# Spectral filter and routed experts on one core: first turn of the last batch moved ahead, bias product on 128 rows, other banks, start loads, blank writes and tail regrouped

## Chip, cores and metric

One Trainium2 chip, one core of it. The metric is the device time of one execution in microseconds (us), smaller is better; several executions are timed and their median is given. One further execution was taken by the hardware profiler; its own time stands beside its span.

## What is computed

The reference, cut to its two stages (`D = 256`, 8 batches of 2,496 tokens; 8 experts, hidden size 1,024):

```python
def _attn_ref(x, w_r, w_i, b_r, b_i):          # x: (8, 2496, 256)
    X = np.fft.rfft(x, axis=1)
    Yr = Xr @ w_r - Xi @ w_i + b_r
    Yi = Xr @ w_i + Xi @ w_r + b_i
    Yr = np.sign(Yr) * np.maximum(np.abs(Yr) - 0.01, 0.0)   # Yi alike
    return np.fft.irfft(Yr + 1j * Yi, n=2496, axis=1)

def _moe_ref(x, w_gate, w1, w2):               # x: (19968, 256)
    expert_idx = np.argmax(x @ w_gate, axis=1)
    for e in range(8):
        xe = x[expert_idx == e]
        out[expert_idx == e] = gate_w[:, None] * (np.maximum(xe @ w1[e], 0) @ w2[e])
```

`gate_w` is the softmax probability of the chosen expert. All of it is float32.

## The kernel before, in words

**Spectral stage.** The transform of length 2,496 is done as 39 x 64, with matmuls by constant matrices. A batch is worked in 10 "turns" of 2 frequencies each; 8 x 10 = 80 iterations `it` of one loop in `spectral` go through them, software-pipelined: in an iteration PE, the TensorE queue, does the forward product of the next turn (`fwd_b`, tile `pb` from the loaded `t` and the basis `bm`), the second inverse product of an older one (`inv_b`, tile `pv` from `y` and the basis `bi`), the products by the weights (`mix`: `pk`, then `pm`, written as sums of float32r halves `whr`, `wlr`, `sh`, `sl`), the first forward products of the next batch (`fwd_a`, tile `pa`) and last inverse products of the batch before (`inv_a`, which is `inv_z` with tile `pz` and, one piece behind, `inv_y` with tile `py`). Tables `first`, `loads`, `back` and `pieces` say which of these stand in which `it`. VectorE (DVE) and ScalarE (ACT) work between the products: ACT copies `k` from `pk` in the last batch (DVE adds in the others), DVE sums `v` from `pm` and `k`, ACT makes `r` and DVE `y` (the soft threshold), ACT copies `z` from `pv`, `zh` and DVE `zl` are the halves of `pz`, ACT copies `yb` from `py`. In the last batch the bias is added inside `pm` by one more matmul (line 355), whose stationary operand `ones` and moving operand `bias_r` have 33 partitions.

**Experts.** A route job (DVE and ACT steps on `lg`, `mx`, `scan`, ...) finds each token's expert and place; rows are scattered to `xs` in DRAM by POOL (GpSimd), and 82 tiles of 256 tokens then go through `up` (tile `ph`) and `down` (tile `po`), with an indirect store to `out` by POOL. The first `BUSY = 7` tiles are mixed with the end of the last batch in `finish_last`; `breathe` there gives the jobs in hand three steps between two pieces of matmuls, one of these jobs being `table(1)`, which computes the table of the late tiles and ends with the product `pl` from `lap`. The last `RARE = 3` tiles stand in an If each, read from the table (`live`); with these data none is taken.

**What sets the order.** PE, ACT, DVE and SP (the queue that issues the hardware DMAs) run in the order in which the code is written (`manual_schedule`), so a wait of one instruction holds all behind it on its engine. PSUM banks come from pools: `psf` has one bank "b" (`pb`) and one "m" (`pk` and `pm`), `psi` has a ring "u" of four (`pa`, `pv`, `pz`) and a pair "yo" (`py`, `pn`, `pq`, `pl`). `write_blank` has POOL issue 8 DMAs of 270 KB that put an empty tile ahead of every expert's rows.

Of the kernel before, what the change touches and what calls it, by code (L numbers as in the profile page):

```python
# [100 lines left out]
class Kernel:  # L101
# [71 lines left out]
    def open_forward(self, st):  # L173
        tc, nc, nb = self.tc, self.nc, self.nb
        f = self.f = self.pool(st, "f", 1, side="right")
        self.xst = ExitStack()
        self.xp = self.pool(self.xst, "xp", 4)
        self.tp = self.pool(st, "tp", 6, side="right")
        self.w = self.pool(st, "w", 2, side="right")
        self.psf = self.pool(st, "psf", 1, side="right", space=PSUM)  # L180

        y = [self.w.tile([128, 2, D], F32, tag="y", name=f"first{i}", bufs=3) for i in range(2)]
        self.idle, self.row1, self.brow = y[0][:, 0, :].bitcast(BF16), y[0][0:1, 1, 0:128], y[1][0:1]
        nc.vector.memset(self.idle, 0.0)
        nc.vector.memset(self.row1, 1.0)
        self.far = far = f.tile([117, 120], F32, name="far")
        self.fer = f.tile([78, 120], F32, name="fer")
        nc.sync.dma_start(far, self.c_fa)
        self.bm = f.tile([128, K1, 128], F32, name="bm")
        self.bi = f.tile([128, K1, 128], F32, name="bi")  # L190
        self.bias = f.tile([128, 2, D], F32, name="bias")
        self.bias_r = f.tile([33, 2, D], F32R, name="bias_r")
        self.ones = f.tile([33, 128], F32R, name="ones")
        self.xg = {}
        for q in range(6):
            self.load_x(0, q)
        nc.sync.dma_start(self.fer, self.c_fe)
        self.wh, self.wl = {}, {}
        self.raw = {}
        self.nlam = f.tile([128, 1], F32, name="nlam")  # L200
        nc.vector.memset(self.nlam, -LAM)

        nc.gpsimd.dma_start(self.gar, self.c_ga)
        for c in range(2):
            nc.gpsimd.dma_start(self.iw[:, c, c * 128:c * 128 + 8], self.w_gate[c * 128:(c + 1) * 128, :])
        nc.gpsimd.dma_start(self.ids, self.c_ids)
        nc.gpsimd.dma_start(self.score, self.c_score)
        nc.gpsimd.dma_start(self.base, self.c_base)
        nc.gpsimd.dma_start(self.ltri_f, self.c_ltri)
        nc.gpsimd.dma_start(self.tcol, self.c_tcol)  # L210
        for z in self.zs:
            nc.gpsimd.memset(z[:, :, 64:66, :], 0.0)
# [48 lines left out]
    def split_bias(self, part):  # L261
        nc = self.nc
        if part == 0:
            nc.scalar.activation(self.bias_r[0:32], self.bias[0:32], AF.Copy, scale=self.tcol[0:32, 2:3])
        elif part == 1:
            bh = self.w.tile([33, 2, D], F32R, tag="y", name="bh", bufs=3)
            nc.scalar.copy(bh[32:33], self.bias[32:33])
            nc.vector.tensor_sub(self.bias_r[32:33], self.bias[32:33], bh[32:33])
        else:
            nc.scalar.activation(self.ones, self.ident[0:33], AF.Copy, scale=0.0, bias=1.0)  # L270

# [73 lines left out]

    def mix(self, b, s):
        nc = self.nc
# [23 lines left out]
        yield  # L371
        if b or s:
            p = self.psf.tile([128, 2, D], F32, tag="m", name="pm", bufs=1)
        else:
            p = self.psi.tile([128, 512], F32, tag="u", name="pm", bufs=4).rearrange("p (a d) -> p a d", a=2)
# [22 lines left out]
    def inv_b(self, b, s):  # L398
        nc = self.nc
        y = self.ys.pop((b, s))  # L400
        p = self.psi.tile([128, 512], F32, tag="u", name="pv", bufs=4).rearrange(
            "p (c a r n) -> p c a r n", c=2, a=2, r=2)
        for kp in range(2):
# [12 lines left out]
    def inv_z(self, b, i):  # L416
        nc = self.nc
        for g in (2 * i, 2 * i + 1) if i < GH else ():
# [7 lines left out]
            nc.scalar.copy(h, p[:120, :YW])  # L426
            nc.vector.tensor_sub(l, p[:120, :YW], h)
            self.hl[g] = h, l
# [14 lines left out]
    def spectral(self, fwd):  # L443
# [7 lines left out]
        for i, pair in enumerate(pairs):  # L451
            self.fwd_a(0, *pair)
            if i == 4:
                self.load_basis("bm", 0, 2)
                self.load_w("r")
# [5 lines left out]
        self.turn(0, 1)  # L461
        self.load_basis("bm", 2, 6)
        self.turn(0, 2)
        if nb > 1:
            self.load_x(1, 0)
        self.turn(0, 3)
        self.load_basis("bi", 0, 4)
        self.keep_warm(12)
# [8 lines left out]
        for b in range(1, nb):  # L477
            at = 10 * b - 10
            for i, o in enumerate((1, 2, 2, 3, 3, 4, 4, 5, 5, 6, 6) if b == 1 else (-3, -2, -1, 0, 0, 1, 2, 3, 4, 5, 6)):
                first[at + o].append((b, *pairs[i]))  # L480
# [12 lines left out]
        for it in range(n):  # L493
# [10 lines left out]
            if it:  # L504
                small = self.shrink(*todo[it - 1])
                next(small)
            mix = self.mix(b, s)
            next(mix)
# [10 lines left out]
            self.tick(1)  # L519
            self.nudge()  # L520
            for a in pieces[it][:1]:
                self.inv_a(*a)
            next(mix, None)
            self.tick(3 if it >= n - 5 else 1)
            self.nudge()
# [3 lines left out]
            for a in pieces[it][1:]:  # L529
                self.inv_a(*a)  # L530
            for a in loads[it]:
                self.load_x(*a)
            if it == 3:
                self.split_inverse()
            if 6 < it < 10:
                self.split_bias(it - 7)
            if it == 6:
                self.write_blank(self.us[b, s][0:1, 0, 0:1])
            if it < 4:
                self.load_basis(*(("bm", 6, 12), ("bi", 4, 10), ("bm", 12, 20), ("bi", 10, 20))[it])  # L540
            if it + 4 < n and (it != 6 or nb == 1):
                if it == 7:
                    self.turn(*todo[it + 3])
                self.turn(*todo[it + 4])
# [16 lines left out]
        for _ in self.inv_b(*todo[n - 1]):  # L561
            pass
        self.inv_y(nb - 2, 9)
        self.inv_y(nb - 2, 10)
        self.pace(self.yb[0:1, GH - 1, 8:9])
# [24 lines left out]
    def breathe(self):  # L590
        self.tick(3)

    def finish_last(self):
        tiles = itertools.chain.from_iterable(self.step(t) for t in range(BUSY))
        fill = itertools.chain(self.first1(), self.first2())
        for i in range(GH + 1):
            self.inv_a(self.nb - 1, i)
            if i:
# [11 lines left out]
            self.breathe()  # L610
        self.jobs.append(self.table(1))
        for _ in tiles:
            self.breathe()
# [91 lines left out]
    def table(self, last):  # L705
# [82 lines left out]
        if last:  # L788
            lap = rt.tile([128, 128], F32, name="lap")
            nc.vector.tensor_copy(lap, fin[:, 3:4].broadcast_to((128, 128)))  # L790
            for _ in range(4):
                yield
# [225 lines left out]
    def experts_rest(self, late):  # L1018
        late.enter_context(self.tc.manual_schedule(engines={mybir.EngineType.Activation, mybir.EngineType.DVE}))
        main = self.nt - RARE  # L1020
        for t in range(BUSY, main):
            for _ in self.step(t):
                pass
        live = self.nc.values_load(self.tabs[1][0:1, 3, 0:1], min_val=0, max_val=self.nt)  # L1024
        nt = self.nt
        for t in range(main, nt):
            with self.tc.If(live > t - self.early):
                if t > main:
# [29 lines left out]
```

## Time and profile before

| | |
|---|---|
| timed runs | 1549.34, 1551.67, 1552.24 us; median 1551.67 us |
| profiled execution | 1549.26 us, span 1547.4 us |
| mean granted clock of TensorE | 0.995 |
| PE busy / weight loads | 1512.6 us (98%) / 1383.2 us (89%) |
| DVE / ACT / POOL busy | 957.2 us (62%) / 759.0 us (49%) / 392.5 us (25%) |
| spectral loop | from about 32 to 566 us of the span |
| steady state of the experts | from about 700 us on, with PE busy 800.0 of 800 us to 1500 |

Busy time of PE is the union of its matmuls' spans, whose ends are modelled and overlap; a pause of PE therefore is read from the start times. The clock column (PEclk) is 1.00 at 2.4 GHz and 0.50 at 1.2 GHz, or a mean between them. "Idle before" in a row counts from the modelled end of the matmul before it.

### The profile page before, as it was taken

How to read it: one execution, taken by the hardware profiler on the slowest of the kernel's cores; microseconds unless marked ns; L12 is line 12 of the kernel's file. 1: busy time of each engine (PE TensorE's matmuls, PEld its weight loads, DVE VectorE, ACT ScalarE, POOL GpSimd, SP SyncE). 2: the span in 40 equal slices, each digit the busy share in tenths (PEclk: the TensorE clock that was granted, in tenths of full speed). 3: DMA queues.
4: the chain of work that ended last, by engine and by line, in shares of the span. 5: the costliest groups of instructions: out<-in, count | busy, mean ns of one | idle time of the engine just before them, and what ended most of it. 6: DMA issues, size and time to landing. Idle time of an engine off the chain costs nothing. (4 is left out here: it accounts for less than half of the span.)

```text
span 1547.4 us, 35414 instructions
## 1 busy us (share of the span) xinstructions
PE 1512.6 (98%) x10808; PEld 1383.2 (89%) x10808; DVE 957.2 (62%) x2178; ACT 759.0 (49%) x1629; POOL 392.5 (25%) x550
## 2 busy tenths in 40 slices
PE   8999999999999999999999999999999999999997
PEld 3779899999898889899999999999999999999996
DVE  3778888889898777745555455454545445445442
ACT  2666766767666565434444434343434334334332
POOL 1100243343444453333421111111111111111111
PEclk9999999999999999999999999999999999999999
DMA  7954455555543332434443323232314124132210
GB/s 227 269 177 115 132 169 149 151 165 153 156 143 118 108 78 54 114 90 104 120 115 97 99 53 93 56 94 64 85 42 105 43 50 100 43 82 65 50 42 20
DMA packets 194726, 162.03 MB, mean 105 GB/s; under 512 B 127868, under 2 KB 164516, under 8 KB 194513
## 3 DMA queue, kind: packets, MB, share of 16 engines
q1 hardware_dynamic: 174705, 115.53, 29.2%
q0 software_dynamic: 19808, 44.03, 8.4%
q8 instruction: 88, 1.44, 0.4%
q14 instruction: 125, 1.02, 0.2%
HBM read 241.99 MB, written 66.37 MB: 199 GB/s over the span
## 5 line engine op out<-in xcount | busy, mean ns | idle before, releaser
L986 PE MATMUL po<-h,hh 128*128 128x512 f32 x1312 | 461.9, 395 | 0.0
L949 PE MATMUL ph<-xh,h 128*128 128x256 f32 x1312 | 372.0, 284 | 1.1 <-DVE hl L955 1.0
L949 PE MATMUL ph<-xl,h 128*128 128x256 f32 x1312 | 371.1, 283 | 0.0
L949 PE MATMUL ph<-xh,l 128*128 128x256 f32 x1312 | 370.7, 283 | 0.0
L983 PE MATMUL po<-h,hl 128*128 128x256 f32 x1148 | 323.9, 282 | 0.0
L955 DVE SCALAR_TENSOR_TENSOR hl<-ph,hh 128x512 fp32r<-128x512 f32 x328 | 226.1, 689 | 147.4 <-ACT hh L954 95.0
L954 ACT ACTIVATE hh<-ph 128x512 fp32r<-128x512 f32 x328 | 193.7, 598 | 205.5 <-PE ph L949 197.8
L986 PEld LDWEIGHTS po<-h,hh 128*128 128x128 f32 x1312 | 241.5, 188 | 43.4
L995 POOL DMA_INDIRECT out<-o,row x124 | 123.2, 994 | 581.6 <-DVE o L993 479.0
L993 DVE SCALAR_TENSOR_TENSOR o<-po,xr,part 128x256 f32<-128x256 f32 x156 | 75.4, 484 | 302.3 <-ACTq L911 153.7
L949 PEld LDWEIGHTS ph<-xh,l 128*128 128x128 f32 x1312 | 251.2, 191 | 3.7
L949 PEld LDWEIGHTS ph<-xh,h 128*128 128x128 f32 x1312 | 251.2, 191 | 2.5 <-DVE hl L955 2.1
L949 PEld LDWEIGHTS ph<-xl,h 128*128 128x128 f32 x1312 | 251.2, 191 | 0.0
L992 ACT ACTIVATE part<-po,xr 128x256 f32<-128x256 f32 x156 | 73.8, 473 | 334.5 <-PE po L986 318.3
L983 PEld LDWEIGHTS po<-h,hl 128*128 128x128 f32 x1148 | 215.5, 188 | 6.0 <-DVE hl L955 1.6
L690 POOL DMA_INDIRECT xs_dram<-yb,pos x176 | 179.8, 1021 | 103.5 <-issue 55.8
L392 DVE SCALAR_TENSOR_TENSOR y<-v,r 64x256 f32<-64x256 f32 x320 | 133.4, 417 | 5.0 <-ACT r L386 0.8
L421 PEld LDWEIGHTS pz<-iw,z 128*120 128x120 f32 x704 | 90.7, 183 | 22.2 <-issue 22.1
L421 PE MATMUL pz<-iw,z 128*120 128x136 f32 x704 | 96.7, 280 | 0.0
L409 ACT COPY z<-pv 128x256 f32<-128x256 f32 x160 | 92.7, 700 | 2.1 <-PE pa L293 1.4
L326 PE MATMUL pb<-bm,t 128*128 128x128 f32 x640 | 85.4, 276 | 5.1 <-DMA t<-spec_dram 2.8
L337 ACT COPY re<-pb 128x256 f32<-128x256 f32 x80 | 29.6, 370 | 116.8 <-PE pb L326 102.7
(183 smaller groups left out, 2556.7 us busy)
## 6 DMA issues: line engine op xcount, KB each, us to landing
r<-moe_w SPq DMA_DIRECT2D x672, 128.0 KB
r<-moe_w SPq DMA_DIRECT2D x166, 512.0 KB
xq<-xs_dram SPq DMA_DIRECT2D x332, 64.0 KB
t<-spec_dram SPq DMA_DIRECT2D x160, 128.0 KB
spec_dram<-ae SPq DMA_DIRECT2D x78, 240.0 KB
x<-x SPq DMA_DIRECT2D x40, 384.0 KB
x<-x SPq DMA_DIRECT2D x40, 84.0 KB
xs_dram<-yb,pos POOLq DMA_INDIRECT x176
```

The source lines that it names most:

```text
L326: nc.tensor.matmul(p[:, c, :, kp, :], t[:, kp, c * 128:(c + 1) * 128], self.bm[:, 2 * s + kp, :], start=True, stop=True)
L392: nc.vector.scalar_tensor_tensor(out=y[q * 64:q * 64 + 64, kp, :], in0=u[h, q, :], scalar=LAM, in1=r[h, q, :], op0=ALU.add, op1=ALU.min)
L409: nc.scalar.copy(self.zs[b % 2][:, c, 0:NB, 4 * s:4 * s + 4].rearrange("p n a -> p a n"), p[:, c].rearrange("p a r n -> p (a r) n"))
L421: nc.tensor.matmul(p[:120, c * 136:(c + 1) * 136], self.zs[b % 2][:, c, 3 * g:3 * g + 3, :].rearrange("p j a -> p (j a)"), self.iw[:, c, : ...
L690: i = nc.gpsimd.indirect_dma_start(out=self.xs[:, :], out_offset=bass.IndirectOffsetOnAxis(ap=pos[:n, g:g + 1], axis=0), in_=y[:n, g, 0:XW ...
L949: nc.tensor.matmul(p[:, i, :], a[:, c, f * 128:(f + 1) * 128], v[:, c, :], start=m == 0, stop=m == 5)
L954: nc.scalar.activation(hh[:, s, :], p, AF.Relu)
L955: nc.vector.scalar_tensor_tensor(out=hl[:, s, :], in0=p, scalar=0.0, in1=hh[:, s, :], op0=ALU.max, op1=ALU.subtract)
L983: nc.tensor.matmul(p[:, :D], hl[:, f - 1, hs], w2[:, f - 1, 0, :], start=False, stop=False)
L986: nc.tensor.matmul(p, hh[:, f, hs], w2[:, f].rearrange("p a d -> p (a d)"), start=f == 0, stop=f == 7)
L993: nc.vector.scalar_tensor_tensor(out=o[:, h, :], in0=p[:, :D], scalar=xr[:, h, 0:1], in1=part, op0=ALU.mult, op1=ALU.add)
L995: i = nc.gpsimd.indirect_dma_start(out=self.out[:, :], out_offset=bass.IndirectOffsetOnAxis(ap=at[h], axis=0), in_=o[:, h, :], in_offset=N ...
```

## The change

Twelve edits, in the order of the code:

- `bias_r` and `ones` get 128 partitions instead of 33, the added ones of `bias_r` being filled through column 2 of `tcol`.
- `mix` takes `alone`: for `it` 0 and 1, and in the last batch for its turns 2 and 9 (`it` 72 and 79), `pm` stands in a bank of ring "u" instead of in bank "m", where `pk` stands. Before, this was so for `it` 0 alone.
- `inv_b` of the very last turn puts `pv` into bank "b" instead of ring "u".
- `inv_z` takes `held`: in `it` 76 to 79 the two `zl` of an iteration's first piece are issued behind `v` instead of ahead of it.
- The start loads: the basis `bm` comes as 0:4, 4:8, 8:12 (was 0:2, 2:6, 6:12), `turn(0, 3)` and the basis `bi` 0:4 ahead of `load_x(1, 0)`, and in `it` 0 to 3 the basis loads (in `it` 0 the turn's too) ahead of the x loads.
- `fwd_a` of batch 1: its first piece moves from `it` 1 to 2, and so on.
- `write_blank` moves from `it` 6 to 11.
- `inv_z(7, 0)`, first of the last batch, moves ahead of `inv_y(6, 10)`, last of the batch before.
- `breathe` gives two steps instead of three when only `table(1)` is left, and `table(1)` takes 7 steps instead of 4 between `lap` and `pl`.
- The rare tiles stand in one If with all three in it, and `live` is read ahead of tile 7 by all engines but POOL.

```diff
-        self.bias_r = f.tile([33, 2, D], F32R, name="bias_r")
-        self.ones = f.tile([33, 128], F32R, name="ones")
+        self.bias_r = f.tile([128, 2, D], F32R, name="bias_r")
+        self.ones = f.tile([128, 128], F32R, name="ones")
...
-            nc.scalar.activation(self.bias_r[0:32], self.bias[0:32], AF.Copy, scale=self.tcol[0:32, 2:3])
+            nc.scalar.activation(self.bias_r, self.bias, AF.Copy, scale=self.tcol[:, 2:3])
...
-        if b or s:
+        if not alone:
             p = self.psf.tile([128, 2, D], F32, tag="m", name="pm", bufs=1)
...
+        if (b, s) == (self.nb - 1, 9):
+            p = self.psf.tile([128, 2, 2, 2, 64], F32, tag="b", name="pv", bufs=1)
...
-            nc.vector.tensor_sub(l, p[:120, :YW], h)
+            if self.held is None:
+                nc.vector.tensor_sub(l, p[:120, :YW], h)
+            else:
+                self.held.append((l, p[:120, :YW], h))
...
-                self.load_basis("bm", 0, 2)
+                self.load_basis("bm", 0, 4)
...
-        self.load_basis("bm", 2, 6)
+        self.load_basis("bm", 4, 8)
         self.turn(0, 2)
+        self.turn(0, 3)
+        self.load_basis("bi", 0, 4)
         if nb > 1:
             self.load_x(1, 0)
-        self.turn(0, 3)
-        self.load_basis("bi", 0, 4)
...
-            for i, o in enumerate((1, 2, 2, 3, 3, 4, 4, 5, 5, 6, 6) if b == 1 else (-3, -2, -1, 0, 0, 1, 2, 3, 4, 5, 6)):
+            for i, o in enumerate((2, 2, 3, 3, 4, 4, 5, 5, 5, 6, 6) if b == 1 else (-3, -2, -1, 0, 0, 1, 2, 3, 4, 5, 6)):
...
-            mix = self.mix(b, s)
+            mix = self.mix(b, s, it < 2 or b == nb - 1 and (not pieces[it] or pieces[it][0][1] == 0))
...
+            self.held = [] if it >= n - 4 else None
             for a in pieces[it][:1]:
                 self.inv_a(*a)
             next(mix, None)
+            for to in self.held or ():
+                self.nc.vector.tensor_sub(*to)
+            self.held = None
...
-            if it == 6:
+            if it == 11:
                 self.write_blank(self.us[b, s][0:1, 0, 0:1])
...
         self.inv_y(nb - 2, 9)
+        self.inv_z(nb - 1, 0)
         self.inv_y(nb - 2, 10)
...
-        self.tick(3)
+        self.tick(2 if len(self.jobs) == 1 and self.last_table else 3)
...
-            self.inv_a(self.nb - 1, i)
+            if i:
+                self.inv_a(self.nb - 1, i)
...
-            for _ in range(4):
+            for _ in range(7):
                 yield
...
+        live = self.nc.values_load(self.tabs[1][0:1, 3, 0:1], min_val=0, max_val=nt)
         for t in range(BUSY, main):
             for _ in self.step(t):
                 pass
-        live = self.nc.values_load(self.tabs[1][0:1, 3, 0:1], min_val=0, max_val=self.nt)
-        nt = self.nt
-        for t in range(main, nt):
-            with self.tc.If(live > t - self.early):
+        with self.tc.If(live > main - self.early):
+            for t in range(main, nt):
```

Order of ACT at the end of the last batch, before, from `r` of the last turn (`z_106<-pv`: last turn; `zh`, `yb`: last pieces of the batch before, then `zh` of the last batch; `xh`: first tile of the experts):

```order
L386 ACTIVATE r<-v,nlam 128x512
L409 COPY z_106<-pv 128x4x64 x2
L426 CAST zh<-pz 120x272 x2
L439 COPY yb<-py 117x272 x2
L426 CAST zh<-pz 120x272 x2
L409 COPY z_106<-pv 128x4x64 x2
L439 COPY yb<-py 117x272 x4
L426 CAST zh<-pz 120x272 x2
L927 CAST xh_8391<-xf 128x512
```

The same place after (lines are those of the changed code):

```order
L386 ACTIVATE r<-v,nlam 128x512
L412 COPY z_106<-pv 128x4x64 x2
L429 CAST zh<-pz 120x272 x2
L445 COPY yb<-py 117x272 x2
L429 CAST zh<-pz 120x272 x2
L412 COPY z_106<-pv 128x4x64 x2
L445 COPY yb<-py 117x272 x2
L429 CAST zh<-pz 120x272 x2
L445 COPY yb<-py 117x272 x2
L943 CAST xh_8391<-xf 128x512
```

The first `zh` of the last batch now stand between the two last pairs of `yb` of the batch before; nothing else has moved.

Order of DVE in `it` 77, before (`y`: the turn before, `zl`: a piece of the batch before, `v`: this turn, then a route job):

```order
L392 SCALAR_TENSOR_TENSOR y<-v,r 64x256 x2
L653 TENSOR_REDUCE sm<-ex 117x11
L427 TENSOR_TENSOR zl<-pz,zh 120x272 x2
L379 TENSOR_TENSOR v<-pm,k 128x512
L655 TENSOR_SCALAR sm<-sm 117x11
L656 RECIPROCAL yb<-sm 117x11
```

The same place after:

```order
L392 SCALAR_TENSOR_TENSOR y<-v,r 64x256 x2
L669 TENSOR_REDUCE sm<-ex 117x11
L379 TENSOR_TENSOR v<-pm,k 128x512
L532 TENSOR_TENSOR zl<-pz,zh 120x272 x2
L671 TENSOR_SCALAR sm<-sm 117x11
L672 RECIPROCAL yb<-sm 117x11
```

`v` now stands ahead of the two `zl`; `it` 76 and 78 read alike.

Order of POOL at the very end, before (`ISA` at the If's line: POOL adds to semaphores in place of the branch that isn't taken; the last `ISA` is the end of the program):

```order
L1027 COMPARE_AND_BRANCH
L911 UNCONDITIONAL_BRANCH
L995 DMA out<-o,row 19968x256 x2
L1027 UNCONDITIONAL_BRANCH
L1027 ISA
L1027 UNCONDITIONAL_BRANCH
L1027 COMPARE_AND_BRANCH
```

The same place after:

```order
L1041 COMPARE_AND_BRANCH
L927 UNCONDITIONAL_BRANCH
L1011 DMA out<-o,row 19968x256 x2
L919 UNCONDITIONAL_BRANCH
L927 UNCONDITIONAL_BRANCH
L1011 DMA out<-o,row 19968x256 x2
L919 UNCONDITIONAL_BRANCH
L927 UNCONDITIONAL_BRANCH
L1011 DMA out<-o,row 19968x256 x2
L1041 UNCONDITIONAL_BRANCH
L1041 ISA
```

Before, the piece shown stands three times, each with an `ISA` for two stores that are passed over; after, one `ISA` stands for all six.

## Rows read from the trace of the kernel before

**Rows 1.** The page: busy time, share of the span and instructions

```profile
PE 1512.6 (98%) x10808; PEld 1383.2 (89%) x10808; DVE 957.2 (62%) x2178; ACT 759.0 (49%) x1629; POOL 392.5 (25%) x550
```

**Rows 2.** Windows: us, busy us by engine, PEclk, DMA share, GB/s

```profile
60.00:80.00 20.00, 19.62 (x135) 15.98 (x134) 15.24 (x32) 14.17 (x31) 5.02 (x11) 1.00 0.94 287
100.00:120.00 20.00, 20.00 (x158) 18.52 (x157) 16.65 (x37) 13.61 (x34) 0.00 (x0) 1.00 0.46 132
495.00:563.00 68.00, 66.37 (x504) 60.79 (x502) 54.98 (x158) 42.90 (x112) 29.41 (x48) 1.00 0.37 101
700.00:1500.00 800.00, 800.00 (x5621) 748.05 (x5621) 402.50 (x710) 315.91 (x580) 159.23 (x171) 1.00 0.30 77
```

**Rows 3.** Window 580 to 584, same columns

```profile
580.00:584.00 4.00, 3.84 (x20) 3.50 (x20) 3.86 (x13) 3.65 (x11) 2.47 (x4) 0.57 0.20 62
```

**Rows 4.** Groups of PE by line and shape: busy us, mean ns, idle before

```profile
L355 PE MATMUL pm<-bias_r,ones 33*128 33x256 f32 x20 | 7.6, 381 | 0.8 <-ACT k L366 0.8
```

**Rows 5.** Timeline of PE around a bias product: start us, duration us

```profile
538.14 0.28 PE L359 MATMUL pm<-wld,sh 128*128 128x256 f32 x1
538.26 0.28 PE L359 MATMUL pm<-whd,sl 128*128 128x256 f32 x1
538.47 0.38 PE L355 MATMUL pm<-bias_r,ones 33*128 33x256 f32 x1
538.77 0.39 PE L359 MATMUL pm<-whs,sh 128*128 128x256 f32 x1
539.00 0.28 PE L359 MATMUL pm<-wls,sh 128*128 128x256 f32 x1
```

**Rows 6.** Timelines of POOL, SP and PE around the blank writes

```profile
73.09 4.27 POOL L232 DMA_DIRECT2D xs_dram<-blank  x8 [0.45 <-POOL blank L230]
...
75.71 5.79 SPq L313 DMA_DIRECT2D t<-spec_dram  x4
...
83.55 1.13 PE L326 MATMUL pb<-bm,t 128*128 128x128 f32 x8 [2.04 <-DMA t<-spec_dram]
```

**Rows 7.** Timelines of PE and DVE in the first two iterations

```profile
32.62 1.13 PE L326 MATMUL pb<-bm,t 128*128 128x128 f32 x8 [1.12 <-DMA bm<-c_bm]
39.66 0.39 PE L359 MATMUL pm<-whd,sh 128*128 128x256 f32 x1 [1.09 <-DVE k L368]
42.52 1.13 PE L326 MATMUL pb<-bm,t 128*128 128x128 f32 x8 [1.18 <-DMA spec_dram<-ae]
...
33.38 0.41 DVE L343 TENSOR_TENSOR sl<-su,sh 128x256 fp32r<-128x256 f32 x1
40.83 0.85 DVE L392 SCALAR_TENSOR_TENSOR y<-v,r 64x256 f32<-64x256 f32 x2
```

**Rows 8.** Timeline of PE in iteration 72 and the next

```profile
513.69 0.38 PE L355 MATMUL pm<-bias_r,ones 33*128 33x256 f32 x1 [0.25 <-ACT k L366]
518.20 0.36 PE L359 MATMUL pk<-whr,sh 128*128 128x256 f32 x1 [0.20 <-DVE v L379]
```

**Rows 9.** Timeline of PE at the end of the last batch

```profile
563.63 0.38 PE L355 MATMUL pm<-bias_r,ones 33*128 33x256 f32 x1 [0.52 <-ACT k L366]
570.02 1.16 PE L405 MATMUL pv<-bi,y 128*128 128x128 f32 x8 [0.39 <-DVE zl L427]
572.66 0.39 PE L438 MATMUL py<-zh,gh 120*117 120x272 f32 x1 [0.72 <-ACT yb L439]
578.51 0.38 PE L438 MATMUL py<-zh,gh 120*117 120x272 f32 x1 [1.29 <-ACT yb L439]
```

**Rows 10.** Timeline of PE in the first expert tiles

```profile
637.82 0.39 PE L949 MATMUL ph<-xh,h 128*128 128x256 f32 x1 [0.73 <-DVE hl L955]
650.65 0.49 PE L794 MATMUL pl<-ident,lap 128*128 128x128 f32 x2 [1.50 <-DVE lap L790]
```

**Rows 11.** Lines 1027 and 1054: duration ns min/median/max, first and last start us

```profile
L1027 POOLq INC_SWDGE_SEM  x3: 1180/1194/1236, 1538.1 to 1541.0; - x3
L1054 POOLq DRAIN  x3: 46/109/4317, 1542.3 to 1547.1; - x3
```

More of the change, by code (lines that the diff above doesn't have):

```diff
@@ L269, in split_bias @@
         else:
-            nc.scalar.activation(self.ones, self.ident[0:33], AF.Copy, scale=0.0, bias=1.0)
+            nc.scalar.activation(self.ones, self.ident, AF.Copy, scale=0.0, bias=1.0)
     def split_inverse(self):
@@ L344, in halves, with mix @@
         self.ss[b, s] = sh, sl
-    def mix(self, b, s):
+    def mix(self, b, s, alone):
         nc = self.nc
@@ L400, in inv_b @@
         y = self.ys.pop((b, s))
-        p = self.psi.tile([128, 512], F32, tag="u", name="pv", bufs=4).rearrange(
-            "p (c a r n) -> p c a r n", c=2, a=2, r=2)
+        if (b, s) == (self.nb - 1, 9):
+            p = self.psf.tile([128, 2, 2, 2, 64], F32, tag="b", name="pv", bufs=1)
+        else:
+            p = self.psi.tile([128, 512], F32, tag="u", name="pv", bufs=4).rearrange(
+                "p (c a r n) -> p c a r n", c=2, a=2, r=2)
         for kp in range(2):
@@ L426, in inv_z @@
             nc.scalar.copy(h, p[:120, :YW])
-            nc.vector.tensor_sub(l, p[:120, :YW], h)
+            if self.held is None:
+                nc.vector.tensor_sub(l, p[:120, :YW], h)
+            else:
+                self.held.append((l, p[:120, :YW], h))
             self.hl[g] = h, l
@@ L530, in spectral @@
                 self.inv_a(*a)
+            if it < 4:
+                self.load_basis(*(("bm", 8, 12), ("bi", 4, 10), ("bm", 12, 20), ("bi", 10, 20))[it])
+            if not it:
+                self.turn(*todo[4])
             for a in loads[it]:
@@ L536, in spectral @@
                 self.split_bias(it - 7)
-            if it == 6:
+            if it == 11:
                 self.write_blank(self.us[b, s][0:1, 0, 0:1])
-            if it < 4:
-                self.load_basis(*(("bm", 6, 12), ("bi", 4, 10), ("bm", 12, 20), ("bi", 10, 20))[it])
-            if it + 4 < n and (it != 6 or nb == 1):
+            if 0 < it < n - 4 and (it != 6 or nb == 1):
                 if it == 7:
@@ L595, in finish_last @@
         fill = itertools.chain(self.first1(), self.first2())
+        self.last_table = False
         for i in range(GH + 1):
-            self.inv_a(self.nb - 1, i)
+            if i:
+                self.inv_a(self.nb - 1, i)
             if i:
@@ L611, in finish_last @@
         self.jobs.append(self.table(1))
+        self.last_table = True
         for _ in tiles:
@@ L1019, in experts_rest @@
         late.enter_context(self.tc.manual_schedule(engines={mybir.EngineType.Activation, mybir.EngineType.DVE}))
-        main = self.nt - RARE
+        main, nt = self.nt - RARE, self.nt
+        live = self.nc.values_load(self.tabs[1][0:1, 3, 0:1], min_val=0, max_val=nt)
         for t in range(BUSY, main):
```

## Prediction

> **What bounds the kernel now.** I read the page first: PE is busy in 98% of the span, DVE in 62% [rows 1]. Then the windows: from 700 to 1500 us PE is busy in all of 800 us [rows 2], and the edits leave those tiles' instructions as they are, so nothing is to be had there. What can be had is PE's pauses before 700, extra time within its products, and the end, where PE is done. Then the timeline of PE, where I compared starts: back to back, these matmuls start 0.12 us apart (538.14, 538.26) [rows 5], so a start that comes later holds a pause or a cost of its own. "Idle before" in a row is some 0.1 to 0.2 us shorter than the pause, since a matmul's modelled 0.28 outlasts its 0.12; I count pauses by starts. The clock is not the bound: 1.00 in nearly every window, 0.57 in one of 4 us [rows 2, 3].
>
> **The change part by part**, against the profiled execution's own 1549.26 us.
>
> *Bias on 128 rows: 5.5 us.* The bias product has 33 rows, its neighbours 128. From the start of the matmul ahead of it to that of the second behind it, 538.26 to 539.00, it is 0.74 us for three steps [rows 5]. Three steps between 128-row matmuls would be 0.36, so one bias product costs 0.38 too much, partly ahead of it and partly behind it (the next matmul takes 0.39 like it). There are 20 [rows 4], in the ten turns of the last batch. 16 belong to turns 0 to 7, which makes 16 x 0.38 = 6.1; the four of turns 8 and 9 are in the end of the batch below. If the chain around PE can't follow, less: DVE is busy 54.98 of 68.00 us there [rows 2], 81%, and that work in 62 us would be 89%. That leaves room, but a wait here and there will show. Bounds for a full effect 4 and 6.1; I take 5.5, near the rows. What excludes nothing is another cause: the extra could come from the bank or the new group and not from the rows. Then the term is 0; it is a rival below. The Trainium skill has a page for either side. "TensorEngine Tiling (Array Packing)", section Key Properties, says that a change of tiling mode drains TensorE: by that the 33-row product is a mode change there and one back, which fits a loss on both sides, 6.1 in all. "TensorE: Matmul & The Clock Gate", section LDWEIGHTS (loading the stationary operand), says that a load's time hangs on columns, not on contracted rows: by that alone widening saves nothing, 0 in all, and the late starts of [rows 5] would be unexplained.
>
> *Blank writes at iteration 11: 2.2 us.* POOL issued its 8 blank DMAs from 73.09 to 77.4; in that stretch the DMA engines are 94% busy, and four loads of `t` issued from 75.71 took 5.79 us on SP; `pb` then began at 83.55 after an idle 2.04 [rows 6], 2.2 by starts. At iteration 11, five iterations later and so near 100 us, the DMA share is lower (0.46 [rows 2]), and each `t` is issued three iterations ahead of its use, not the one or two that iteration 7 has for the first turns of batch 1. Bounds: 1.5, if some loads still come late, and 2.3; I take 2.2.
>
> *Start loads, `pm` of iteration 1 in ring "u", first piece of batch 1 later: 0.8 us.* Three pauses: 32.62 (1.12, `pb` for `bm`), 39.66 (1.09, `pm` for `k`, because `pk` and `pm` share bank "m"), 42.52 (1.18, `pb` for its load) [rows 7]. The first gives nothing by itself: the third `pk` behind it needs `sl`, which ends at 33.79 on DVE whatever `pb` does [rows 7]. Without the other two, `pv` must wait for `y`, at 40.83 + 0.85 = 41.68 [rows 7]; before it began some 0.97 behind 42.52 (eight starts of 0.12), at 43.49, but then `pb` already lay behind it. That is at most 1.7. One piece of `pa` that lay in these pauses now runs later at its full cost, so at least 0, and I take the middle.
>
> *`pm` of iteration 72 in ring "u": 0.8 us.* Its bias waits for ACT's `k` at 513.69, and the next `pk` for DVE's `v` in bank "m" at 518.20 (0.25 and 0.20 idle, 0.4 each by starts) [rows 8]. Both waits are for bank "m"; bounds 0 and 0.8.
>
> *End of the last batch: 1.65 us.* Here stand turns 8 and 9 (four bias products, 1.5 at most; `pm` of the last turn in ring "u"), `v` ahead of `zl`, `pv` in bank "b", and the first turn ahead. The pauses are 563.63 (0.52), 570.02 (0.39), 572.66 (0.72) and 578.51 (1.29) [rows 9]. With `pm` early, `y` of turn 8 and the chain `v`, `r`, `y` of turn 9 come next, and they run through DVE and ACT: I expect `pv` of the last turn near 568.4 instead of 570.02, 1.65 earlier. The products of the first turn fill the pause at 572.66, where `py` waits for ACT's `yb`. What they win is asked back at 578.51, where ACT, not PE, is behind: the same copies stand ahead of that `yb`, in another order. So I book nothing for the reordering itself; bounds 0.5 and 2.5. The dip to half clock at 580 to 584 [rows 3] stays with the pause.
>
> *`table(1)` in smaller steps, `pl` three steps later: 0.6 + 1.8 us.* `ph` at 637.82 waited 0.73 for DVE's `hl`, behind three steps of the table; with two steps the table's work reaches less far ahead of `hl`. Bounds 0 and 1.0, middle 0.6. `pl` at 650.65 waited 1.50 for `lap` [rows 10], 1.8 by starts. Three steps later there are dozens of matmuls more ahead of `pl` on PE, far more than 1.8 us, so it goes whole; below 1.2, if the longer job meets a tile's wait.
>
> *One If for the rare tiles: 2.9 us.* Nothing of the matmuls is behind it: POOL, at the very end, adds to semaphores three times, 1.18 to 1.24 us each, first at 1538.1, last at 1541.0, so one in 1.46; then a DRAIN of 4.32 us from 1542.3 and the end [rows 11]. Two of three go: 2 x 1.46 = 2.9. If the cost goes by the semaphores added to (two each before, six in one after), only the branches are saved, 0.3; if the drain's end hangs on something else, as little. I take 2.9, since no row shows a cost for each semaphore. `live` read earlier stalls each queue once, in a place where all have work queued: 0.
>
> **Sum:** 5.5 + 2.2 + 0.8 + 0.8 + 1.65 + 0.6 + 1.8 + 2.9 = 16.25 us, and 1549.26 - 16.25 = 1533.0. The profiled execution lies 2.4 below the median of 1551.67 and 1.3 below the mean of all four times (1550.6); from that mean the sum gives 1534.4, so I say 1534.
>
> **The rivals.**
>
> *The rows are not the cause* of the bias's extra: no 5.5, and less at the end of the batch, about 10 us in all, 1541. For it: `ones` is a new weight in a new group, and its load isn't ahead. Against: other new groups in the timeline start at once, and the matmul behind the bias pays too [rows 5].
>
> *DVE or ACT becomes the bound of the last batch.* DVE at 89% with waits in a fixed order takes back about half of the bias term and some of the end: 16.25 - 3.5 = 12.7, 1538. For it: the pauses of [rows 8, 9] are waits for just these engines. Against: only one to two tenths of a us in an iteration, now.
>
> *The tail stays.* One addition to six semaphores takes three times as long, or the drain ends where it ended: 0.3 instead of 2.9, 1537.
>
> *Slower: the clock.* If new spacing of the matmuls made TensorE fall to 1.2 GHz, each us there would cost half a us of PE-bound work. The dip seen cost 0.43 x 4 = 1.7 us [rows 3]; ten such dips more would eat the 16 us, and from about twelve on the kernel is slower than before by over 0.2%. Against: it came with PE's pause at 578.51, and the change makes pauses fewer; the 800 us of the experts run at 1.00 [rows 2].
>
> **Chances.** As reckoned 0.48; DVE or ACT the bound 0.20; tail stays 0.14; rows not the cause 0.10; several of these three together with a late start, so that under 0.2% is left, 0.05; clock 0.03. All but the last two are faster by more than 0.2% (3.1 us, about what a measurement of this kernel can tell from no change): faster 0.92, same 0.05, slower 0.03. The lower end of the range takes all upper bounds (6.1, 2.3, 1.7, 0.8, 2.5, 1.0, 1.8, 2.9: 19.1, so 1531.5) less 2 for how runs scatter: 1529. The upper end takes in each rival that is faster, 1541, and 1 more: 1542.
>
> **What would show it.** Right: bias products 0.28 long with starts 0.12 apart; `pb` near 83 without a pause; the pauses at 513, 518, 563 and 650 gone; one addition of some 1.2 us on POOL, and the end 2.9 us nearer to the last matmul. Wrong: bias products that still begin 0.2 behind the matmul ahead of them (rows not the cause); new waits for `k`, `v` or `zl` in the last batch (DVE or ACT the bound); an addition of over 3 us, or a longer drain (tail); PEclk under 1.00 over several windows (clock). A pause of `pb` near 100 us would show that the blank writes only moved their cost, up to the 2.2 that I booked.

## The result, and the profile after

The changed kernel takes 1537.12 us (median of 6 runs, 1536.01 to 1537.90), the kernel before 1550.69 us in the same comparison: ratio 0.9912, 95% interval 0.9899 to 0.9925, so 0.9% faster, 13.6 us (11.6 to 15.7). The forecast was 1534 (1529 to 1542). The profiled execution after is the slowest of its six (1537.9 us, span 1536.1); the one before (1549.26, span 1547.4) is faster than all six of the kernel before in this comparison. So the two profiles lie only 11.3 us apart, and the accounts below are made of these.

The page of the profile after, first line of its busy times; it answers to [rows 1]:

```profile
PE 1505.2 (98%) x10808; PEld 1381.0 (90%) x10808; DVE 955.7 (62%) x2178; ACT 758.9 (49%) x1629; POOL 392.2 (26%) x550
```

PE does the same 10808 matmuls in 7.4 us less. Where this comes from is read from starts of the same matmul in both traces (timeline of PE, us):

```
place (a matmul's start)               before    after   ahead by
first pk of iteration 6                 66.94    66.45       0.48
first pk of iteration 9                 85.33    82.56       2.77
first pk of iteration 70               499.10   496.21       2.89
first pk of iteration 78               556.21   548.67       7.54
first pk of iteration 79               562.14   554.53       7.61
py, fifth piece of the last batch      589.00   579.32       9.68
ph, first of tile 1                    608.29   598.54       9.75
ph, first of tile 6                    671.09   662.48       8.61
last matmul                           1535.73  1527.19       8.54
end of the span                       1547.4   1536.1       11.3
```

So 0.5 came at the start, 2.3 with the blank writes, 4.7 in turns 0 to 7 of the last batch, 2.1 at its end, then 1.1 was lost in the first expert tiles, and 2.7 came behind the last matmul. Two of these hold a stretch at half clock that comes and goes between executions, as is shown further on: 0.8 of the 2.1 is one in the profile before, and the 1.1 lost is one of 1.4 in the profile after. The timeline of PE after, around a bias product (start, duration); it answers to [rows 5]:

```profile
532.23 0.28 PE L359 MATMUL pm<-whd,sl 128*128 128x256 f32 x1
532.35 0.28 PE L355 MATMUL pm<-bias_r,ones 128*128 128x256 f32 x1
532.46 0.28 PE L359 MATMUL pm<-whs,sh 128*128 128x256 f32 x1
532.58 0.28 PE L359 MATMUL pm<-wls,sh 128*128 128x256 f32 x1
```

From 532.23 to 532.58 are 0.35 us for three steps, where before there were 0.74. The extra is wholly gone. The loads of the stationary operands (PEld) at the same places, before and then after:

```profile
538.47 0.18 PEld L355 LDWEIGHTS pm<-bias_r,ones 33*128 33x128 f32 x1
538.77 0.19 PEld L359 LDWEIGHTS pm<-whs,sh 128*128 128x128 f32 x1
...
532.23 0.19 PEld L355 LDWEIGHTS pm<-bias_r,ones 128*128 128x128 f32 x1
532.35 0.19 PEld L359 LDWEIGHTS pm<-whs,sh 128*128 128x128 f32 x1
```

A load took as long before as after, but before, the load of the 33-row operand began together with its matmul (538.47), and so did the load behind it (538.77). After, each begins 0.12 us, one step, ahead of its matmul (532.23 and 532.35, 532.35 and 532.46). All 20 bias products of the trace before read so; after, 17 of 20 and every load behind them read as here.

`pb` and the blank writes, PE and POOL after, which answer to [rows 6]:

```profile
80.74 0.28 PE L359 MATMUL pm<-whs,sl 128*128 128x256 f32 x1
80.86 1.05 PE L326 MATMUL pb<-bm,t 128*128 128x128 f32 x8
...
99.51 4.26 POOL L232 DMA_DIRECT2D xs_dram<-blank  x8 [0.45 <-POOL blank L230]
```

`pb` follows at once; the writes take as long at 99.5 (4.26) and no pause stands behind them. New or longer pauses after (timeline of PE and DVE; idle before and its releaser in brackets):

```profile
512.66 0.71 PE L408 MATMUL pv<-bi,y 128*128 128x128 f32 x4 [0.32 <-DVE y L392]
519.29 0.39 PE L444 MATMUL py<-zl,gh 120*117 120x272 f32 x1 [0.71 <-DVE zl L431]
569.67 0.38 PE L444 MATMUL py<-zh,gh 120*117 120x272 f32 x1 [1.75 <-ACT yb L445]
639.28 0.39 PE L965 MATMUL ph<-xh,h 128*128 128x256 f32 x1 [1.75 <-DVE hl L971]
...
636.13 2.50 DVE L914 TENSOR_TENSOR h<-r,h 128x512 fp32r<-128x512 f32 x4
638.55 0.68 DVE L971 SCALAR_TENSOR_TENSOR hl<-ph,hh 128x512 fp32r<-128x512 f32 x1
```

In the last batch, PE now waits for DVE's `y` and `zl`; at 569.67 for ACT, longer than before (1.29 in [rows 9]); and at 639.28 for `hl`, which DVE does behind the four parts of a weight split. That last pause was not there: before, `pl` had one of 1.50 at the same tile [rows 10]. A window after, behind that pause (columns as in [rows 2]):

```profile
640.00:644.00 4.00, 4.00 (x22) 3.95 (x21) 2.54 (x8) 1.19 (x3) 0.71 (x1) 0.57 0.42 84
```

The granted clock is 0.57 there on the mean, a stretch at 1.2 GHz, as it was at 580 to 584 before [rows 3]. At the end stand these lines of POOL, which answer to [rows 11]:

```profile
L1041 POOLq INC_SWDGE_SEM  x1: 1237/1237/1237, 1529.7 to 1529.7; - x1
...
L1069 POOLq DRAIN  x3: 46/109/4317, 1531.0 to 1535.8; - x3
```

One addition to six semaphores takes 1.24 us, as long as each of the three additions to two semaphores that stood there before; the drain is 4.32 us as before and begins 1.3 us behind the addition's start, as before. The span ends 8.9 us behind the last matmul's start, not 11.7: 2.7 us less.

### The profile page after: what moved, and what is told of

It is laid out like the page before. It is cut to its first block, busy times and chain, and to the rows that moved or that the text cites. A ratio compares the mean times of both kernels' runs of the same rounds, so it can differ in the third digit from the quotient of the medians.

```text
span 1536.1 us, 35386 instructions
## 1 busy us (share of the span) xinstructions
PE 1505.2 (98%) x10808; PEld 1381.0 (90%) x10808; DVE 955.7 (62%) x2178; ACT 758.9 (49%) x1629; POOL 392.2 (26%) x550
## 5 line engine op out<-in xcount | busy, mean ns | idle before, releaser
L408 PE MATMUL pv<-bi,y 128*128 128x128 f32 x640 | 85.8, 276 | 1.4 <-DVE y L392 1.1
```

Source lines behind the costliest of these rows:

```text
L408: nc.tensor.matmul(p[:, c, kp, :, :], y[:, kp, c * 128:(c + 1) * 128], self.bi[:, 2 * s + kp, :], start=True, stop=True)
```

## Experiments

Three kernels start from the kernel before and take one edit; the others start from the changed kernel and undo or alter one or two; the last is the changed kernel unaltered. Ratios are to the kernel before, timed in the same comparison, and times in us that follow a ratio are worked out from it.

**The bias product on 128 rows, alone** (lines 192, 193, 264 and 270 of the kernel).

> The kernel before with the bias product on 128 rows and nothing else. If the 33 rows are what costs, the 20 bias products start 0.12 us behind the matmul ahead of them, the pause on either side is gone, and the time is 4.5 to 6.5 us shorter (ratio 0.9958 to 0.9971), a bit under 20 x 0.38 = 7.6 because DVE and ACT give some waits back. If the new group or its weights are what costs, the starts stay 0.2 and 0.3 us apart and the ratio is 1.000.

Measured: 1544.93 us, ratio 0.9967 (0.9955 to 0.9979). So the rows are the cause: 5.1 us in the time (3.3 to 7.0). In the trace iterations 70 to 77 take 53.28 us (501.37 to 554.65) instead of 57.11, so 3.83 less, not 16 x 0.38 = 6.1; the four products of the last two turns give some 0.6 more (25.43 against the tail-alone kernel's 26.01 from the first `pk` of iteration 79 to the fifth piece). Timeline of PE in this run:

```profile
515.18 0.39 PE L355 MATMUL pm<-bias_r,ones 128*128 128x256 f32 x1 [0.69 <-ACT k L366]
519.69 0.36 PE L359 MATMUL pk<-whr,sh 128*128 128x256 f32 x1 [0.80 <-DVE v L379]
554.65 0.36 PE L359 MATMUL pk<-whr,sh 128*128 128x256 f32 x1 [0.58 <-DVE sm L655]
```

The two pauses of [rows 8] grew from 0.25 and 0.20 to 0.69 and 0.80, and a new one of 0.58 came: these three hold 1.6 of the missing 2.3. By starts of `pk`, five of the eight iterations gain 0.76 to 0.79, the full price of two products; all that is missing is in iterations 71 (0.43 gained), 72 (0.44 lost) and 77 (0.05 lost).

**The tail alone** (the last hunk of the diff).

> The kernel before with the last three tiles in one If and the early read of the count, nothing else. If each addition to POOL's semaphores costs the same for two or six, one of 1.2 us stands where three did and the time is 2.9 us shorter (ratio 0.9981). If the cost goes by the semaphores, one addition of some 3.6 us and a gain of at most 0.3 us. If the early read stalls a queue, a new pause of PE at the seventh tile, near 690 us.

Measured: 1546.85 us, ratio 0.9983 (0.9974 to 0.9991), 2.6 us (1.4 to 4.0). POOL's lines of this run:

```profile
L1025 POOLq INC_SWDGE_SEM  x1: 1237/1237/1237, 1540.0 to 1540.0; - x1
```

The cost is one for each such instruction and not for each semaphore. No pause stands near the seventh tile.

**The blank writes alone** (`if it == 11`).

> The kernel before with the blank writes at iteration 11 and nothing else. If the pause of 2.2 us at 83.5 comes from the blank writes alone, it is gone and the time 2.2 us shorter (ratio 0.9986); if the transfers only move their cost, a pause of pb near 100 to 110 us takes its place and the ratio is 1.000.

Measured: 1547.26 us, ratio 0.998 (0.997 to 0.9989), 3.1 us (1.7 to 4.7). In the trace the first `pk` of iteration 8 stands level with that of before (77.82 and 77.81), that of iteration 9 is 2.28 us ahead (83.05 and 85.33), and those up to iteration 30 keep 2.3 to 2.4: gone, and not paid elsewhere.

The price of this pause differs between executions. Two other profiles have the blank writes where the kernel before has them; this is the tail-alone kernel's:

```profile
85.85 0.63 PE L326 MATMUL pb<-bm,t 128*128 128x128 f32 x2 [2.88 <-DMA t<-spec_dram]
...
86.00:90.00 4.00, 4.00 (x22) 4.00 (x23) 1.02 (x2) 2.08 (x5) 0.00 (x0) 0.57 0.59 179
```

`pb` idles longer than the 2.04 of [rows 6], and a stretch at half clock follows; the bias-alone kernel's profile has both too (2.40, and 0.57 from 85 to 89). Iterations 6 to 9 take 20.70 and 20.37 us there, 18.39 in the profile of the kernel before and 16.1 wherever the writes were moved. So against these executions the move is worth 2.3 us in one and 4.3 and 4.6 in the two others, and the 3.1 of the time lies between.

**The table's steps as before, in the changed kernel.**

```diff
-        self.tick(2 if len(self.jobs) == 1 and self.last_table else 3)
+        self.tick(3)
...
-            for _ in range(7):
+            for _ in range(4):
```

> The changed kernel with three steps of the table at a time and four steps between lap and pl, as in the kernel before. By the prediction's terms it is 2.4 us slower than the changed kernel (about 1539.5). By what the changed kernel's trace shows, the pause moved from pl to the next product that waits for hl, behind DVE's four parts of the split of the second weights: then the pause of some 1.7 to 1.9 us stands at pl again, and the time is within 1 us of the changed kernel's 1537.1.

Measured: 1536.05 us, ratio 0.9913 (0.9898 to 0.9928): no difference from the changed kernel. Timeline of PE, then of DVE:

```profile
627.80 0.39 PE L965 MATMUL ph<-xh,h 128*128 128x256 f32 x1 [0.74 <-DVE hl L971]
640.42 0.49 PE L810 MATMUL pl<-ident,lap 128*128 128x128 f32 x2 [1.30 <-DVE lap L806]
...
636.21 2.50 DVE L914 TENSOR_TENSOR h<-r,h 128x512 fp32r<-128x512 f32 x4
638.63 0.68 DVE L971 SCALAR_TENSOR_TENSOR hl<-ph,hh 128x512 fp32r<-128x512 f32 x1
639.23 0.70 DVE L937 STREAM_TRANSPOSE xf<-xq 128x512 f32<-128x512 f32 x1
639.85 0.38 DVE L802 CAST tab<-pq 1x264 int32<-1x264 f32 x1
640.16 0.20 DVE L806 COPY lap<-fin 128x128 f32<-128x128 f32 x1
```

`lap` is a step of 0.20 us, but the split and `hl` stand ahead of it on DVE, and the `ph` behind `pl` needs that same `hl`. `hl` is done at 639.31 (638.63 + 0.68), 1.1 us ahead of `pl`; without `pl` in this place, PE would have stood until then, some 0.35 us from the end of its last step (638.84 + 0.12). That the changed kernel stands longer goes, by the traces, with where the table's other work went. Around the same tile, PE with the table as before, then DVE with the table as before and in the changed kernel:

```profile
635.03 1.03 PE L800 MATMUL pq<-ident,fin 128*1 128x128 f32 x8
...
635.71 0.48 DVE L1009 SCALAR_TENSOR_TENSOR o<-po,xi,part 128x256 f32<-128x256 f32 x1 [0.68 <-ACT part L1008]
...
635.28 0.48 DVE L1009 SCALAR_TENSOR_TENSOR o<-po,xi,part 128x256 f32<-128x256 f32 x1
635.68 0.16 DVE L782 TENSOR_SCALAR n<-n 128x8 f32<-128x8 f32 x1
635.75 0.16 DVE L784 TENSOR_SCALAR te<-te 128x8 f32<-128x8 f32 x1
635.95 0.17 DVE L785 TENSOR_TENSOR st<-te,n 128x8 f32<-128x8 f32 x1
```

With the table as before, the table's eight products `pq` occupy PE for 0.97 us ahead of the tile's first `ph` (636.00), and the split follows `o` at once (636.21). In the changed kernel `pq` comes only at 646.74, and three steps of the table stand between `o` and the split (636.13). So `hl` ends 4.95 us behind the last `po` (634.28 to 639.23) instead of 4.60 (634.71 to 639.31), and PE has 0.97 us less to do until then. By starts the pause is 1.9 us instead of 1.5.

The other edit of the two did its work. The pause of 0.74 at 627.80, which answers to 637.82 in [rows 10], is gone from the changed kernel:

```profile
627.36 0.39 PE L965 MATMUL ph<-xh,h 128*128 128x256 f32 x1
```

In all it comes to nothing: from the first `ph` of tile 2 to the last matmul are 915.12 us here (610.41 to 1525.53) and 915.16 in the second profile of the changed kernel (610.67 to 1525.83), both without half clock.

**The split of the second weights behind the first `hl`, and spread.**

```diff
-        if t:
+        if t >= BUSY:
             self.split2(t)
...
+            if f2 == 0 and 0 < t < BUSY:
+                self.split2(t)
```

> The changed kernel with the split of the second weights in tiles 1 to 6 issued behind the first hl of the tile instead of ahead of it. If the pause at 639 us is hl queued behind the split on DVE, it goes (1.9 us), and the 3.4 us at half clock that follow it (1.7 us) go too if they come from the pause: 2 to 3.6 us faster than the changed kernel, 1533.5 to 1535. If the split is what the tile needs in any order, the wait goes to the po products, which need the split weights, and the time is the same within 1 us or longer.

Measured: 1538.17 us, ratio 0.9927 (0.9914 to 0.994). The pause went on to the next product that waits for `hl`, and grew:

```profile
643.64 0.39 PE L965 MATMUL ph<-xh,h 128*128 128x256 f32 x1 [2.37 <-DVE hl L971]
```

With one part ahead of each `hl`:

```diff
-        if t:
+        if t >= BUSY:
             self.split2(t)
+        elif t:
+            with self.changed(t):
+                self.part2(0)
...
+            if f2 < 3 and 0 < t < BUSY:
+                with self.changed(t):
+                    self.part2(f2 + 1)
+                if f2 == 2:
+                    self.weights(t + 1, 2)
```

> The changed kernel with the four parts of the split of the second weights of tiles 1 to 6 one ahead of each hl, each in an If of its own, instead of all four ahead of the first. DVE's hl of 0.68 and a part of 0.63 fit into PE's 1.43 us for a product group, so if the lump ahead of the first hl is the cause of the pause at 639 us (1.9 us), no such pause is left: 1.5 to 2 us faster than the changed kernel, 1535 to 1535.6, or 3.6 if the half clock that followed it went with the pause. If DVE has too much work there in any order, as the run with all parts behind the first hl hints, the pause is spread over several hl and the sum stays at 1.9 or grows.

Measured: 1535.90 us, ratio 0.9912 (0.9898 to 0.9925). At this tile two smaller pauses are left, and two more stand in earlier tiles, behind the branch of an If on DVE (DVEq):

```profile
615.13 0.38 PE L968 MATMUL ph<-xh,h 128*128 128x256 f32 x1 [0.27 <-DVEq L977]
627.61 0.39 PE L968 MATMUL ph<-xh,h 128*128 128x256 f32 x1 [0.46 <-DVEq L977]
637.94 0.39 PE L968 MATMUL ph<-xh,h 128*128 128x256 f32 x1 [0.16 <-DVE hl L974]
640.20 0.39 PE L968 MATMUL ph<-xh,h 128*128 128x256 f32 x1 [0.56 <-DVE hl L974]
```

The sum is 1.45, where one pause of 1.75 stood; one more of 0.29 behind a branch, at 602.96, stands where the changed kernel has one of 0.31 for `hl`. From the first `ph` of tile 0 to that of tile 5 are 75.34 us (573.17 to 648.51), against 75.57 in the second profile of the changed kernel (573.65 to 649.22). Spreading the work moved most of the pause and removed little of it.

**Banks and `zl` of the last batch as before, in the changed kernel.**

```diff
-            mix = self.mix(b, s, it < 2 or b == nb - 1 and (not pieces[it] or pieces[it][0][1] == 0))
+            mix = self.mix(b, s, it < 2)
...
-        if (b, s) == (self.nb - 1, 9):
+        if False:
...
-            self.held = [] if it >= n - 4 else None
+            self.held = None
```

> The changed kernel with pm of iterations 72 and 79 in bank m again, pv of the last turn in ring u and zl ahead of v: the wide bias product, the first turn ahead and all else stay. By the prediction's terms 0.8 (iteration 72) and most of 1.65 (end) come back: 2 to 2.4 us slower than the changed kernel's 1537.1, with pauses for k and v near 509, 514 and 557. If DVE's chain through y is what bounds the last batch, the pauses for y that the changed kernel shows (0.5, 0.3 and 0.4 us) go in exchange and the loss is under 1 us.

Measured: 1539.03 us, ratio 0.9923 (0.9906 to 0.994), 1.7 us more than the changed kernel by the ratios; the intervals overlap. Iterations 69 to 77 take 59.06 us (491.14 to 550.20) instead of 58.24 (490.43 to 548.67): 0.8 for iteration 72 and `held`. What the end of the batch loses isn't shown, since a stretch at half clock lies in it in this profile (573.5). The pauses for `k` and `v` are back, the one for `y` at 512 is gone:

```profile
510.74 0.39 PE L355 MATMUL pm<-bias_r,ones 128*128 128x256 f32 x1 [0.69 <-ACT k L366]
515.23 0.36 PE L359 MATMUL pk<-whr,sh 128*128 128x256 f32 x1 [0.79 <-DVE v L379]
```

**The first turn not ahead** (`inv_z(nb - 1, 0)` taken out and `if i:` with it).

> The changed kernel with the first turn of the last batch behind the last products of the batch before, as in the kernel before. The prediction booked nothing for this order by itself: the pause of py near 565 (0.9 us) comes back and the later pause for ACT's yb, 1.9 us in the changed kernel, falls to 1.5, so 0.4 to 0.7 us slower than the changed kernel's 1537.1, too little to be timed but to be seen from the starts. If the order is worth what the filled pause shows, 0.9 us or more.

Measured: 1536.65 us, ratio 0.9912 (0.9897 to 0.9927). By the timeline of PE both pauses of [rows 9] are as before:

```profile
563.09 0.38 PE L444 MATMUL py<-zh,gh 120*117 120x272 f32 x1 [0.72 <-ACT yb L445]
568.94 0.38 PE L444 MATMUL py<-zh,gh 120*117 120x272 f32 x1 [1.30 <-ACT yb L445]
```

2.02 in the two, against the changed kernel's one of 1.75: a gain of some 0.3 at most, which no run can tell. The expected loss of 0.4 or more does not show in the time.

**The first forward piece in iteration 1 again.**

```diff
-(2, 2, 3, 3, 4, 4, 5, 5, 5, 6, 6) if b == 1
+(1, 2, 2, 3, 3, 4, 4, 5, 5, 6, 6) if b == 1
```

> The changed kernel with the first forward piece of batch 1 in iteration 1 again. If that piece (two products, 0.86 us) lies in the pauses for y of the first two iterations (0.3 and 0.8 us in the changed kernel), it costs nothing there, and the full iteration 5 with its pause of 0.8 us before pa at 62.4 gets its piece off: 0.9 to 1.7 us faster than the changed kernel, 1535.4 to 1536.2. If the start is bound by the chain through y, the same within 0.3 us.

Measured: 1537.54 us, ratio 0.9918 (0.9903 to 0.9933), and my expectation of a gain was wrong:

```profile
39.77 0.99 PE L293 MATMUL pa<-x,far 117*120 117x512 f32 x1 [1.80 <-DMA x<-x]
```

The basis loads now stand ahead of the x loads on SP, so in iteration 1 the piece's x isn't there. So in the trace the piece had to move for the loads to move; the time shows neither gain nor loss.

**The first tile's transposition earlier** (an idea from the pause at 569.67: ACT sat idle 1.72 us for `xf`, which DVE reached behind three route steps).

```diff
+        fwd.close()
+        self.open_experts(self.late)
+        self.first_up = self.upright(0)
+        next(self.first_up)
         self.inv_y(nb - 2, 9)
         self.inv_z(nb - 1, 0)
         self.inv_y(nb - 2, 10)
```

> The changed kernel with the forward pools closed and the experts' opened ahead of the last two inverse pieces of batch 6, and the first tile's transposition (xf) issued on DVE ahead of zl of the last batch's first turn and ahead of the route steps; its copy xh on ACT stays where it was. In the changed kernel PE waits 1.9 us for yb because ACT sat idle 1.7 us for xf, which DVE reached only behind three route steps at 566.7. If that order is the cause, the pause falls by 1.0 to 1.5 us and the time to about 1536. If ACT's amount of copies is the cause, the pause only moves to the next py, and the time is the same within 0.5 us.

Measured: 1535.57 us, ratio 0.9912 (0.9898 to 0.9925). The timeline of PE has no pause for `yb` there, and one for `zl`:

```profile
568.69 0.38 PE L444 MATMUL py<-zl,gh 120*117 120x272 f32 x1 [0.65 <-DVE zl L431]
```

From the first `pk` of iteration 79 to the fifth piece's `py` (as in the table of starts) are 23.31 us (554.19 to 577.50) instead of 24.79: 1.5 in the trace, as expected, and less than the runs can tell.

With the table's steps as before:

> The early transposition together with the table's steps as in the kernel before (three at a time, four between lap and pl). The first alone left no pause of 1.9 us for yb at the end of the last batch; the second alone cost nothing and its profile had no stretch at half clock at 640. If the two are independent: 1.3 to 1.8 us below the changed kernel, 1535.3 to 1535.8 in the time, with 0.8 us at pl or hl near 626 and 1.6 at pl near 638. If the half clock goes with the pause for hl at 637 and not with one for pl, 1.7 us less on top, about 1534.

Measured: 1536.49 us, ratio 0.9905 (0.989 to 0.9921). Its profile keeps most of the 1.5 (23.46) and has no half clock at 640, but its first `pb` began 2.2 us late (32.61 against 30.38), behind 6.8 us at half clock from 25.2. The ratio is the lowest of all, by 0.0007, which lies well within the intervals. No version here is shown to beat the changed kernel.

**The changed kernel again.**

> The changed kernel, unaltered, with another profile. In five of the profiles so far PE pauses 1.9 us for hl near 640 us and in three of those a stretch of 3.4 us at half clock follows. If the pause brings the stretch each time that the work around it is the same, it stands at 640.6 again and the last product begins near 1527; if it comes and goes between executions of one kernel, it is missing or elsewhere, the pause of 1.9 us is there all the same, and the last product begins up to 1.7 us earlier.

Measured: 1537.19 us, ratio 0.9916 (0.9901 to 0.993). The pause and the window behind it in this profile:

```profile
639.25 0.38 PE L965 MATMUL ph<-xh,h 128*128 128x256 f32 x1 [1.75 <-DVE hl L971]
...
640.00:644.00 4.00, 4.00 (x29) 3.66 (x29) 3.20 (x9) 1.67 (x3) 0.82 (x2) 1.00 0.38 76
```

This is the same kernel with the same pause (1.75 us, ending 0.03 earlier), and a granted clock of 1.00 where it was 0.57. Of the six profiles with this pause, three have the stretch behind it. The first `ph` of the next tile begins at 649.22 instead of 650.62, 1.4 us ahead, and the end is as far ahead (span 1534.8 instead of 1536.1).

## Why the prediction was right, and where it was not

*Bias on 128 rows.* That the rows are the cause is shown: the late starts on both sides are gone in two kernels, with this edit alone and with all. What fails with 33 rows is seen in the loads: they begin with their matmul and not one step ahead. Why they do is not shown. The Trainium skill says in "TensorEngine Tiling (Array Packing)", section Key Properties, that a change of tiling mode drains TensorE. A loss on both sides fits that, but the page does not say that a 33-row matmul is such a change, and no run here shows it. In "TensorE: Matmul & The Clock Gate", section LDWEIGHTS (loading the stationary operand), the skill says that a load's time goes by columns and not by contracted rows. The trace agrees, with 0.18 us for the load before and 0.19 after. That widening saves nothing does not follow from it, since it is the load's start that moved.

The size was off. "I take 5.5, near the rows" measured 3.8 in turns 0 to 7, under the bound of 4. The rival that DVE or ACT becomes the bound was true in part: 2.3 of 6.1 was taken back, in just the three iterations whose waits for `k`, `v` and a DVE step of the route grew, where I allowed 0.6.

*`pm` of iteration 72*: 0.8 forecast; 4.65 less 3.83 and the run with the banks as before both give 0.8. *Blank writes*: 2.2 forecast, 2.28 measured in the trace, more in other executions. *Tail*: 2.9 forecast, 2.7 in the trace, 2.6 in the time; the rival of a cost for each semaphore is refuted.

*Start*: 0.8 forecast, 0.5 measured, with new pauses for `y` (0.17 and 0.61 near 41 us) and one of 0.68 at 62.4 in the full iteration 5, where `pa` waits for ACT's `ae`. This term is not settled. The changed kernel's second profile has no pause at 62.4, and takes 35.15 us from the first `pb` to the first `pk` of iteration 6 where the first profile takes 36.07; but with the start as it was before, one profile takes 36.56 and the tail-alone kernel's 35.50. No run tries the start's edits alone.

*End of the last batch*: 1.65 forecast, and 2.1 measured, of which 0.84 is the half clock at 580 that was there before and not after. The tail-alone kernel has the same code up to there and the same pause of 1.29, but no such stretch, and took 0.84 less over the same matmuls (565.36 to 591.38 against 562.14 to 589.00). So the edits gave 1.2; the bias products alone give 0.6 of it. The statement that the pause at 578.51 asks back what the first turn wins is borne out (2.02 and 1.75 of idle). "The dip to half clock at 580 to 584 stays with the pause" is wrong: the pause stands there in the tail-alone kernel without the dip.

*`table(1)` and `pl`*: I booked 0.6 + 1.8 = 2.4, and measured was nothing. The 0.6 came (0.74 of idle at 627.80, gone). The step that failed is the 1.8, "it goes whole" because matmuls stand ahead of `pl`: the pause of 1.5 by starts went, and one of 1.9 for `hl` came. I read the releaser of the pause, `lap`, and not what DVE did ahead of `lap`: the split of 2.50 us and `hl`, on which the matmuls behind `pl` wait as well. And I did not ask what the moved work had done where it stood: `pq` had filled 0.97 us of PE's wait for the split, and the steps that moved came to stand ahead of the split. The sums of starts fit this; no run moves `pq` or these steps alone.

*The sum* was 16.25 us. With the terms as measured, 0.5 + 2.3 + 3.8 + 0.8 + 1.2 + 0 + 2.7 is 11.3. The two profiles differ by 11.3, and by 11.8 without the stretches at half clock (0.84 before, 1.4 after). The timed runs say 13.6 (11.6 to 15.7) and, in the last comparison, 13.0 by the ratio 0.9916. The 2.2 us between are the two profiled executions' distances from their medians: 1.4 below before, 0.8 above after. What the other executions did is not on record; the dearer pause at the blank writes in two of three profiles is one thing that can have made the kernel before slower. The time, 1537.1, lies nearer to the rival with DVE or ACT as the bound (12.7 us, 1538) than to the sum (1534). That the forecast came within 3 us is in part luck: its terms were 5 us too high in sum, and the runs fell by 2 us more than the profiles do.

## What to carry to other kernels

A matmul with few contraction rows among full ones can cost more than a full one; here, padding both operands to 128 rows, with zeros in one of them so that the sum stays the same, took the extra away. A pause's releaser is only the last to come: before the pause is booked as gain, look at what its engine did just ahead of it, ask whether the next instruction waits for that too, and ask what the work that is moved away did where it stood. And when PE's own time shrinks in a stage where another engine is 80% busy in a fixed order, a third of the gain may return as waits, as it did here.

## What the runs showed of the hardware

- A 33-row product between 128-row ones cost 0.38 us more than three steps of 0.12: 0.09 ahead of it, 0.19 behind it and 0.10 behind the next. With 128 rows the extra was 0. The 33-row operand's load and the next one began with their matmuls in all 20 cases; with 128 rows they began 0.11 to 0.13 us ahead, but for three of the 20 bias loads of a trace.
- POOL's addition to semaphores at a branch not taken took 1.24 us for six of them and 1.18 to 1.24 us for two.
- The granted clock fell to 0.50 for a stretch of 3.4 us, which cost 1.4 us, in one execution of a kernel and not in another of the same kernel with the same pause ahead of it. A comparison of single profiles carries such differences.
